# RWKV attention into a SoLU feed-forward on one core: a written-out order for the first chunks, constant products on TensorE, one row of u, and a reordered first pair

## The chip, the cores and the metric

The kernel runs on one core of a Trainium2 chip. The time is that of the device in microseconds, from launch to the end of the last instruction; lower is better. The core has five engines with a queue each, worked off strictly in program order: TensorE (PE, matrix products into PSUM), VectorE (DVE), ScalarE (ACT), GpSimd (POOL, which does not touch PSUM here) and SyncE (SP, which issues nearly all DMAs). They meet only through semaphores, so an instruction that waits holds up all that stands behind it on its engine.

## The reference

```python
# attention: r, k, v of shape (4, 8, 768, 48); w, u of shape (8, 48)
for t in range(S):
    cur = einsum('bhd,bhe->bhde', u[None] * kt, vt)
    y[:, :, t] = einsum('bhd,bhde->bhe', rt, state + cur)
    state = w[None, :, :, None] * state + einsum('bhd,bhe->bhde', kt, vt)
x = y.transpose(0, 2, 1, 3).reshape(3072, 384)
# feed-forward: w_in (384, 1024), w_out (1024, 384), g_ln (1024)
h = x @ w_in
e = exp(h - h.max(-1)); sm = e / (e.sum(-1) + 1e-9)
solu = h * sm
ln = (solu - mean(solu)) / sqrt(var(solu) + 1e-6) * g_ln
out = ln @ w_out
```

w_in, w_out and g_ln reach the chip as 64-bit floats and are converted there.

## The kernel before

**Chunks.** A unit of work is one batch and 128 tokens: 4 batches x 6 chunks are 24 units, numbered with the batch running fastest. "Chunk i" below is unit i. Inside a chunk the recurrence is a masked score matrix (r times decay, k times inverse decay, only later rows), plus the diagonal term with u; between chunks a state per batch is carried.

**Steps of a chunk, by name and line.** `load` (L472) brings k and r ("kr") and v. `turn_r` and `turn_k` (products L726 and L734) transpose r and k on TensorE; VectorE multiplies r by a table of powers (L727), ScalarE copies k (L736). `decay_k` and `decay_r` (L682, L689) multiply k and r by a table on GpSimd. `weigh` (L695, L696) forms k*u*r, on GpSimd but for chunk 0, where VectorE does it; `sum_own` (L700) sums it per head on VectorE; `diagonal` (L714) writes eight diagonal matrices on ScalarE. `whole_scores` (L749) are the score products, `take_scores` (L773) copies them under the mask over the diagonals on VectorE. `whole_y` (L800) gives the attention output, `take_y` (L849) copies it on ScalarE into xT, `whole_outer` (L874) gives the chunk's outer product and `update` (L895 to L901) adds it to the state. `ffn_in` (L909) is h = x @ w_in and ScalarE's exponential of it (L912). `unit` takes the reciprocal of the sum (L919), multiplies h by e (L921, VectorE) and centres and squares on ScalarE (L923, L924). `halve_ln` (L959) splits solu into 16-bit halves on ScalarE, `turn` has a DMA transpose them, `join_ln` (L953) puts them together again on VectorE; `ffn_out` (L991) multiplies by w_out, ScalarE scales the result (L993) and SyncE stores it. `deviation` (L930, L932) forms the scale on GpSimd.

**Weights.** They come in 14 pieces: six of w_in (512 KB each, three for each half of h's columns), eight of w_out (384 KB each). `load_weights` (L511) has six buffers. `convert_a` (L522, ScalarE), `convert_b` (L535, L537, VectorE), `convert_c` (L545, GpSimd) and for w_out `convert_d` (L552, VectorE) make 32-bit floats of one piece. For w_in `convert_b` puts its first result, `part`, into h's PSUM tile.

**The first stage** is a loop over i from -2 to 6. Iteration i works ahead: it turns chunk i+2, scores i+1, outputs i, and from i = 2 on runs the feed-forward of j = i-2; a table `conversions` says how many pieces each iteration converts. h of chunk 0 comes at the top of i = 2, with both halves together.

**The second stage** takes pairs of chunks, i = 7, 9, ... In it the scores are computed for 64-token halves: `scores` (L766), `within` (L828, the part of y inside a half), `carried` (L839, the part from the state and from `middle`, L883), `outer` (L865). `attend` does scores, outer, masked copies and `middle` for two chunks. From chunk 9 on k and r are transposed by DMA too: `halve_rk` (ScalarE L973, VectorE L974) splits them, `turn` transposes, `join_rk` (L953) joins. The first pair, i = 7, is marked `late` and has an order of its own: `ffn_in(5)`, `unit(5)` and `attend([7, 8])` first, then the rest of `decay`, then `sum_own(10)` and `halve_rk(10)`; `unit(6)` stands after `join_rk(10)` and `diagonal(10)`.

**PSUM** has eight banks: two for the scores, two for h, two in a ring "m" (y, outer product, o, tables), and one each for "ka" and "kb" (turn_r, turn_k, and the outer products of the pairs).

The order on every engine is that of the Python calls; no scheduler moves anything.

Of the kernel before, what the change touches and what calls it, by code (L numbers as in the profile page):

```python
# [399 lines left out]
def direct_path(  # L400
# [53 lines left out]
    psM = ctx.enter_context(tc.tile_pool(name="psM", bufs=2, space=PSUM))  # L454
# [13 lines left out]
    def load(i, which="krv"):  # L468
        b, c = units[i]
        for t, src, n in ((kpads, k, "k"), (rpads, r, "r"), (vts, v, "v")):  # L470
            if n in which:
# [14 lines left out]
    nc.scalar.dma_start(out=u_bc.rearrange("p h d -> p (h d)"),  # L486
                        in_=u.rearrange("h d -> (h d)").partition_broadcast(128))
# [37 lines left out]
    def convert_b(j):  # L525
        hi, low = step[j]
        n = low.shape[1]
        ma = wpool.tile([128, n], U32, tag="ma", name="ma", bufs=4)
        part = ma
        if pieces[j][2] is None:  # L530
            part = psH.tile([128, dff], F32, tag="h", name="part").bitcast(U32)[:, 0:n]

        nc.vector.tensor_scalar(out=part, in0=hi, scalar1=3, scalar2=0x3FFFFFF8,  # L535
                                op0=ALU.logical_shift_left, op1=ALU.bitwise_and)
        nc.vector.scalar_tensor_tensor(out=ma, in0=hi, scalar=0xC0000000, in1=part,  # L537
                                       op0=ALU.bitwise_and, op1=ALU.bitwise_or)
        step[j] = ma, low
# [30 lines left out]
    load(1, "kr")  # L570
    load_weights(1)
    load(2, "kr")
    load_weights(2)
    load_weights(3)
    load(0, "v")
    load(3, "kr")
    load_weights(4)
    load(1, "v")
    load_weights(5)
    load(4, "kr")  # L580
    load(2, "v")

    ident = const.tile([128, 128], F32, name="ident")
    make_identity(nc, ident)
    for vt in vts:
        nc.gpsimd.memset(vt[:, :, D:], 0.0)
# [21 lines left out]
    nc.tensor.transpose(wd_ps, wq.rearrange("a q d -> a (q d)"), ident[0:HP, 0:HP])  # L608
    nc.vector.tensor_scalar(out=pw[:, 0, 0], in0=wd_ps, scalar1=LOW, scalar2=HIGH,
# [112 lines left out]
    def turn_r(i):  # L722
        rT = factors(i)["rT"]
        ps = psM.tile([128, HP, T], F32, tag="ka", name="tr_ps", bufs=1)
# [4 lines left out]
    def turn_k(i):  # L729
        X = live[i]  # L730
        ps = psM.tile([128, HP, T], F32, tag="kb", name="tk_ps", bufs=1)
# [119 lines left out]
    def outer(chunks):  # L851
# [4 lines left out]
        kv = [psM.tile([128, 2, HP, D], F32, tag=f"k{'ab'[c]}", name="kv_ps", bufs=1)  # L856
# [47 lines left out]
    def ffn_in(i):  # L904
        X = live[i]
        h_ps = psH.tile([128, dff], F32, tag="h", name="h_ps")
        for n in range(dff // NX):
            for j in range(KD):
                nc.tensor.matmul(h_ps[:, ts(n, NX)], X["xT"][:, j, :], w_in_sb[:, j, ts(n, NX)],  # L909
                                 start=(j == 0), stop=(j == KD - 1))  # L910
        e = X["e"] = fpool.tile([128, dff], F32, name="e", bufs=1)
        nc.scalar.activation(out=e, in_=h_ps, func=ACT.Exp, accum_out=sums[:, i : i + 1])  # L912
        X["h"] = h_ps
# [84 lines left out]
    todo = list(range(len(pieces)))  # L998
    conversions = {-2: 1, -1: 1, 0: 2, 1: 2, 2: 2, 3: 2, 4: 2, 5: 2}
    now = []  # L1000
    for i in range(-2, LA + LO):
        j = i - LA
        if i == -1:
            nc.sync.dma_start(out=g_sb, in_=moe_g_ln.rearrange("(c p) -> p c", p=128))
        if 0 <= i:
            load(i + 5, "kr")
            load(i + 3, "v")
        if i >= LA:
            ffn_in(j)
        before, now = now, [todo.pop(0) for _ in range(conversions.get(i, 0))]  # L1010
        for p in before:
            if pieces[p][2] is not None:
                convert_c(p)
        if i == -2:
            turn_r(0)
            turn_k(0)
            turn_table(back, kdec, psM.tile([128, HP, 128], F32, tag="m", name="kd_ps"))
            weigh(0, nc.vector)
            decay_k(0)
            sum_own(0)  # L1020
        for p in now:
            convert_a(p)
            if ahead < len(pieces):
                load_weights(ahead)
                ahead += 1
        if -2 < i:
            turn_r(i + 2)
            if i >= LA:
                unit(j)
            if i < 0 or i >= LA:  # L1030
                sum_own(i + 2)
            turn_k(i + 2)
        if i < LA:
            for p in now:
                convert_b(p)
        if i == 0:
            sum_own(2)
        if i != 1:
            decay_k(i + 3)
            if i + 3 >= FIRST:  # L1040
                decay_r(i + 3)
            if i < 0:
                weigh(i + 3, nc.gpsimd)
        for p in now if i < LA else []:
            convert_c(p)
        if i == 1:
            weigh(3, nc.gpsimd)
            decay_k(4)
        if 1 <= i:
            weigh(i + 3, nc.gpsimd)  # L1050
# [8 lines left out]
        if 0 <= i + 1 < WHOLE:  # L1059
            whole_scores(i + 1)  # L1060
            take_scores(i + 1)
        if i < 0:
            diagonal(i + 2)
        if 0 <= i:
# [4 lines left out]
        if i == 1:  # L1069
            turn_table(fore, rdec, psM.tile([128, HP, 128], F32, tag="ka", name="rd_ps",  # L1070
                                            bufs=1))
            sum_own(3)
        if 0 <= i:
            diagonal(i + 2)
        if i == 1:
            nc.vector.tensor_single_scalar(out=minus_g, in_=g_sb, scalar=-1.0, op=ALU.mult)
        if i >= LA:
            for p in before:
                convert_d(p)
            for p in now:  # L1080
                convert_b(p)
# [28 lines left out]
    for i in range(LA + LO, N + LA + LO, 2):  # L1110
# [10 lines left out]
        if late:  # L1121
            decay(i + 3)
            ffn_in(j)
# [9 lines left out]
        if late:  # L1133
            sum_own(i + 3)
            halve_rk(i + 3)
# [26 lines left out]
        for n in (i, i + 1):  # L1162
            if n < N:
                update(n)
        for n in second:
# [5 lines left out]
        if j + 1 < N:  # L1171
# [57 lines left out]
```

## Time and profile before

| | |
|---|---|
| median of 6 runs | 353.93 us (351.54 to 354.68) |
| profiled execution: time / span | 351.09 us / 349.3 us |
| TensorE busy in the span | 329.4 us (94%) |
| VectorE, ScalarE, GpSimd busy | 206.3, 234.3, 169.1 us |
| DMA traffic | 52.88 MB, mean 151 GB/s |
| first product of h, chunk 0 | 27.63 us |
| first product of h, chunks 1 and 2 | 36.78 and 45.34 us |
| first product of h, chunk 8 | 117.53 us |

The page gives the busy share of each engine in 40 slices, the TensorE clock that was granted ("PEclk", ten tenths shown as 9), the chain of work that ended last, and groups of instructions. An order-of-time line reads: start, time taken, engine, line, operation, output and input tiles and shapes, number of instructions; in square brackets, how long the engine stood idle before it and what ended that. "PEld" is the load of a matrix that stays in the array. A 128x512 product in 32 bits counts as two instructions in the profile. The times of a chunk's steps are those of one execution, the profiled one.

### The profile page before, as it was taken

What the parts mean: (1) busy time and instruction counts of PE and PEld (TensorE: products, weight loads), DVE (VectorE), ACT (ScalarE), POOL (GpSimd) and SP (SyncE); (2) the same over time, 40 slices, a digit from 0 to 9 for tenths busy, and PEclk for the clock granted to TensorE, in tenths of its full rate; (3) what the DMA queues carried; (4) which work ended last, traced back from release to release, by engine and by line L of the source; (5) the groups of instructions that cost most, each with busy time, mean ns of one, the idle gap of its engine ahead of it and who ended that gap; (6) DMA issues with size and microseconds to landing.
All of it is one profiled execution on the core that took longest, in us unless ns stands there. A gap on an engine that the chain in (4) does not pass through costs nothing.

```text
span 349.3 us, 10540 instructions
## 1 busy us (share of the span) xinstructions
PE 329.4 (94%) x4443; PEld 196.0 (56%) x4443; DVE 206.3 (59%) x381; ACT 234.3 (67%) x476; POOL 169.1 (48%) x199
## 2 busy tenths in 40 slices
PE   2599999999999799999999999999999999999993
PEld 2485566656555365565565565565565555555563
DVE  7795888896476389459459369367256062233320
ACT  4765988988854895794794794796595465465510
POOL 4879667799949199466476475450300000000000
PEclk9769999999999999999999999999999999999999
DMA  7999998169999999969979979869823522554641
GB/s 170 262 223 196 258 213 133 29 115 178 145 237 165 173 210 174 194 150 163 158 173 165 164 160 155 147 139 188 187 79 65 129 75 56 127 127 97 136 98 42
DMA packets 164885, 52.88 MB, mean 151 GB/s; under 512 B 157917, under 2 KB 161245, under 8 KB 164829
## 3 DMA queue, kind: packets, MB, share of 16 engines
q1 hardware_dynamic: 164684, 51.92, 78.8%
q8 instruction: 37, 0.61, 0.8%
q10 hardware_dynamic: 144, 0.20, 0.2%
q14 instruction: 20, 0.16, 0.2%
HBM read 26.94 MB, written 4.72 MB: 91 GB/s over the span
## 4 chain that ended last, share of the span: by engine, by line
PE 77%; ACT 6%; DMA 6%; SPq 5%; DVE 3%; issue 2%; POOL 1%; ACTq 0%; DVEq 0%; POOLq 0%
PE o_ps L991 33%; PE h_ps L909 32%; DMA halves<-halves 4%; PE at L828 3%; PE at L839 3%; SPq L472 3%; PE at L766 2%; SPq L511 2%; DMA raw<-in_moe_w_in_dram 2%; DVE solu L921 2%; ACT AT L714 2%; PE kv_ps L865 2%; ACT halves L959 1%; ACT e L912 1%; PE y_ps L800 1%
## 5 line engine op out<-in xcount | busy, mean ns | idle before, releaser
L909 PE MATMUL h_ps<-w_in_sb,xT 128*128 128x512 f32 x288 | 129.8, 600 | 3.7 <-DVE solu L921 3.3
L991 PE MATMUL o_ps<-w_out_sb,lnT 128*128 128x384 f32 (+1 forms) x400 | 128.3, 476 | 0.0
L991 PEld LDWEIGHTS o_ps<-w_out_sb,lnT 128*128 128x128 f32 x400 | 74.3, 190 | 48.9 <-issue 4.3
L909 PEld LDWEIGHTS h_ps<-w_in_sb,xT 128*128 128x128 f32 x288 | 52.8, 190 | 63.4 <-issue 57.2
L912 ACT ACTIVATE e<-h_ps 128x1024 f32<-128x1024 f32 x24 | 24.5, 1022 | 38.0 <-PE h_ps L909 37.9
L923 ACT ACTIVATE solu<-solu,st 128x1024 f32<-128x1024 f32 x24 | 27.5, 1148 | 33.3 <-DVE solu L921 33.3
L959 ACT COPY halves<-solu 128x2048 uint16<-128x2048 uint16 x24 | 45.4, 1892 | 6.0 <-DMA halves<-halves 6.0
L899 POOL TENSOR_TENSOR state<-state,pw 48x192 f32<-48x192 f32 x32 | 22.6, 707 | 49.6 <-DVE state L895 47.8
L953 DVE COPY lnT<-halves 128x2048 uint16<-128x2048 uint16 x24 | 37.7, 1590 | 6.0 <-DMA halves<-halves 5.7
L930 POOL TENSOR_SCALAR st<-st 128x1 f32<-128x1 f32 x24 | 6.4, 265 | 64.2 <-ACT e L924 64.1
L682 POOL TENSOR_TENSOR kp<-kpad,kdec 128x512 f32<-128x512 f32 x24 | 32.0, 1334 | 6.0 <-ACT kdec L631 5.4
L714 ACT ACTIVATE AT<-same,own 128x64 f32<-128x64 f32 x136 | 34.3, 340 | 0.0
L695 POOL TENSOR_TENSOR rku<-kpad,u_bc 128x384 f32<-128x384 f32 x23 | 28.4, 1235 | 9.1 <-DVE own L700 9.1
L919 DVE RECIPROCAL st<-sums 128x1 f32<-128x1 f32 x24 | 3.8, 160 | 47.8 <-ACT e L912 47.5
L921 DVE SCALAR_TENSOR_TENSOR solu<-h_ps,st,e 128x1024 f32<-128x1024 f32 x24 | 30.8, 1284 | 2.1
L565 DVE TENSOR_REDUCE least<-mag 128x1 f32<-128x384 f32 (+1 forms) x14 | 8.5, 606 | 35.0 <-ACT mag L563 35.0
L953 DVE COPY rk<-halves 128x2048 uint16<-128x2048 uint16 x15 | 23.7, 1581 | 7.2 <-DMA halves<-halves 7.0
L696 POOL TENSOR_TENSOR rku<-rku,rpad 128x384 f32<-128x384 f32 x23 | 26.9, 1169 | 1.8
L993 ACT ACTIVATE o<-o_ps,st 128x384 f32<-128x384 f32 (+1 forms) x25 | 14.0, 558 | 18.5 <-PE o_ps L991 12.6
L924 ACT ACTIVATE e<-solu 128x1024 f32<-128x1024 f32 x24 | 25.4, 1057 | 0.8
L689 POOL TENSOR_TENSOR rp<-rpad,rdec 128x512 f32<-128x512 f32 x15 | 21.0, 1402 | 4.3 <-DVE halves L974 4.3
L773 DVE COPY_PREDICATED AT<-later_half,at 128x256 f32<-128x256 uint32 x34 | 12.3, 440 | 14.5 <-PE at L766 14.5
(101 smaller groups left out, 383.0 us busy)
## 6 DMA issues: line engine op xcount, KB each, us to landing
raw<-in_moe_w_in_dram SPq DMA_DIRECT2D x12, 512.0 KB, 4.8
raw<-in_moe_w_out_dram SPq DMA_DIRECT2D x16, 384.0 KB, 4.5
kpad<-in_k_dram SPq DMA_DIRECT2D x24, 192.0 KB, 4.8
rpad<-in_r_dram SPq DMA_DIRECT2D x24, 192.0 KB, 5.5
vt<-in_v_dram SPq DMA_DIRECT2D x24, 192.0 KB, 5.4
out_dram<-o SPq DMA_DIRECT2D x23, 192.0 KB, 3.7
halves<-halves SPq DMA_TRANSPOSE x39, 5.2
u_bc<-in_u_dram ACTq DMA_DIRECT2D x1, 192.0 KB, 3.1
```

Source lines behind the costliest of these rows:

```text
L682: nc.gpsimd.tensor_mul(X["kp"].rearrange("p h d -> p (h d)"), kpads[i % NLD].rearrange("p h d -> p (h d)"), kdec.rearrange("p a d -> p (a ...
L695: engine.tensor_mul(rku, kpads[i % NLD][:, :, 0:D], u_bc)
L696: engine.tensor_mul(rku, rku, rpads[i % NLD][:, :, 0:D])
L714: nc.scalar.activation(out=AT[:, h, :], in_=unit_matrix, func=ACT.Copy, scale=X["own"][:, h])
L909: nc.tensor.matmul(h_ps[:, ts(n, NX)], X["xT"][:, j, :], w_in_sb[:, j, ts(n, NX)], start=(j == 0), stop=(j == KD - 1))
L912: nc.scalar.activation(out=e, in_=h_ps, func=ACT.Exp, accum_out=sums[:, i : i + 1])
L921: nc.vector.scalar_tensor_tensor(out=solu, in0=X["h"], scalar=rs, in1=X["e"], op0=ALU.mult, op1=ALU.mult, accum_out=tot)
L923: nc.scalar.activation(out=solu, in_=solu, func=ACT.Identity, scale=-float(dff), bias=tot)
L924: nc.scalar.activation(out=X["e"], in_=solu, func=ACT.Square, accum_out=ss)
L953: nc.vector.tensor_copy(out=words.bitcast(U16).rearrange("p n (t o) -> p o n t", o=2), in_=turned)
L959: nc.scalar.copy(out=both.rearrange("p (o n) -> p o n", o=2), in_=split(X["solu"]))
L991: nc.tensor.matmul(o_ps, X["lnT"][:, f, :], w_out_sb[:, f, part], start=(f == 0), stop=(f == KF - 1))
```

## The change

**Order.** The iterations -2 to 1 and the feed-forward of chunk 0 are replaced by a list of calls. In it the six pieces of w_in are all converted ahead of the second half of h(0); `ffn_in` takes the halves of h's columns one at a time, the first half after the first four pieces have been converted; the output of chunk 2 and the turns of chunk 3 follow h(0); conversion of w_out begins with iteration 2. Conversions of a piece go through `take_up` (`convert_a`, then the next weight load). `weigh(0)` is on GpSimd.

**Loads.** v of chunk 0 and 1 are issued earlier, k and r of chunk 3 after the sixth weight piece, g_ln at the end of the list.

**Constant products.** `spin(n)` issues n products of the identity by itself into h's PSUM tile, whose result nobody reads; 19 in all, at six places.

**u.** It is loaded as one row; a product with a row of ones spreads it over 128 partitions in PSUM, and ScalarE copies it to `u_bc`.

**PSUM.** "ka", "kb" and "m" become one ring of four banks, into which `part` goes too.

**First pair.** `sum_own(10)` and `halve_rk(10)` stand ahead of `ffn_in(5)`; `unit(6)` stands after the state update, ahead of `join_rk(10)`.

```diff
-    psM = ctx.enter_context(tc.tile_pool(name="psM", bufs=2, space=PSUM))
+    psM = ctx.enter_context(tc.tile_pool(name="psM", bufs=4, space=PSUM))
...
-    nc.scalar.dma_start(out=u_bc.rearrange("p h d -> p (h d)"),
-                        in_=u.rearrange("h d -> (h d)").partition_broadcast(128))
+    u_row = u_bc[0:1].rearrange("p h d -> p (h d)")
+    nc.scalar.dma_start(out=u_row, in_=u.rearrange("h d -> (h d)").unsqueeze(0))
...
-            part = psH.tile([128, dff], F32, tag="h", name="part").bitcast(U32)[:, 0:n]
+            part = psM.tile([128, n], F32, tag="m", name="part").bitcast(U32)
...
     load(1, "kr")
+    load(0, "v")
     load_weights(1)
     load(2, "kr")
     load_weights(2)
+    load(1, "v")
     load_weights(3)
-    load(0, "v")
+    load_weights(4)
+    load_weights(5)
     load(3, "kr")
-    load_weights(4)
-    load(1, "v")
-    load_weights(5)
+    load(2, "v")
     load(4, "kr")
-    load(2, "v")
+    nc.sync.dma_start(out=g_sb, in_=moe_g_ln.rearrange("(c p) -> p c", p=128))
...
+    def spin(n):
+        ps = psH.tile([128, dff], F32, tag="h", name="spin")
+        for _ in range(n):
+            nc.tensor.matmul(ps[:, 0:128], ident, ident, start=True, stop=True)
+    spin(3)
...
+    u_ps = psM.tile([128, dm], F32, tag="m", name="u_ps")
+    nc.tensor.matmul(u_ps, ones_row, u_row, start=True, stop=True)
+    nc.scalar.copy(out=u_bc.rearrange("p h d -> p (h d)"), in_=u_ps)
+    spin(3)
...
-    def ffn_in(i):
+    def ffn_in(i, halves=(0, 1)):
         X = live[i]
-        h_ps = psH.tile([128, dff], F32, tag="h", name="h_ps")
-        for n in range(dff // NX):
+        if 0 in halves:
+            X["h"] = psH.tile([128, dff], F32, tag="h", name="h_ps")
+        h_ps = X["h"]
+        for n in halves:
...
+    turn_r(0)
+    turn_k(0)
+    turn_table(back, kdec, psM.tile([128, HP, 128], F32, tag="m", name="kd_ps"))
+    weigh(0, nc.gpsimd)
+    decay_k(0)
+    sum_own(0)
+    diagonal(0)
+    take_up(0)
+    spin(2)
+    whole_scores(0)
+    convert_b(0)
+    decay_k(1)
+    weigh(1, nc.gpsimd)
+    turn_r(1)
+    spin(4)
+    turn_k(1)
+    take_scores(0)
+    convert_c(0)
+    sum_own(1)
+    take_up(1)
+    diagonal(1)
+    spin(3)
+    whole_y(0)
+    whole_outer(0)
+    convert_b(1)
+    convert_c(1)
+    whole_scores(1)
+    update(0)
+    take_y(0)
+    decay_k(2)
+    weigh(2, nc.gpsimd)
+    turn_r(2)
+    take_up(2)
+    spin(4)
+    turn_k(2)
+    take_scores(1)
+    convert_b(2)
+    convert_c(2)
+    load(5, "kr")
+    load(3, "v")
+    whole_y(1)
+    whole_outer(1)
+    whole_scores(2)
+    take_up(3)
+    take_y(1)
+    convert_b(3)
+    convert_c(3)
+    sum_own(2)
+    ffn_in(0, (0,))
+    take_up(4)
+    convert_b(4)
+    convert_c(4)
+    load(6, "kr")
+    load(4, "v")
+    take_up(5)
+    diagonal(2)
+    convert_b(5)
+    convert_c(5)
+    ffn_in(0, (1,))
+    update(1)
+    take_scores(2)
+    decay_k(3)
+    whole_y(2)
+    whole_outer(2)
+    turn_r(3)
+    take_y(2)
+    turn_k(3)
+    unit(0)
+    weigh(3, nc.gpsimd)
+    decay_k(4)
+    turn_table(fore, rdec, psM.tile([128, HP, 128], F32, tag="m", name="rd_ps"))
+    update(2)
+    sum_own(3)
+    diagonal(3)
+    weigh(4, nc.gpsimd)
+
+    todo = list(range(6, len(pieces)))
     now = []
-    for i in range(-2, LA + LO):
+    for i in range(LA, LA + LO):
...
         if late:
             decay(i + 3)
+            sum_own(i + 3)
+            halve_rk(i + 3)
             ffn_in(j)
             unit(j)
             attend([i, i + 1])
...
-        if late:
-            sum_own(i + 3)
-            halve_rk(i + 3)
...
         for n in (i, i + 1):
             if n < N:
                 update(n)
+        if late:
+            unit(j + 1)
         for n in second:
             join_rk(n)
...
-        if j + 1 < N:
+        if j + 1 < N and not late:
             unit(j + 1)
```

## The prediction

> **What bounds the kernel now.** I read the page's slices first, then the busy time by stretch, then the chain that ended last, then the order of time at the start and in the first pair. Slices:
>
> ```profile
> PE   2599999999999799999999999999999999999993
> PEclk9769999999999999999999999999999999999999
> DMA  7999998169999999969979979869823522554641
> ```
>
> TensorE is full but for the start, slice 14 and the end. By stretch (length, then busy us and count of PE, PEld, DVE, ACT, POOL, then granted clock, DMA share, GB/s):
>
> ```profile
> 10.00:15.00 5.00, 2.88 (x40) 2.33 (x40) 3.00 (x6) 4.06 (x12) 4.82 (x5) 0.85 1.21 265
> 15.00:20.00 5.00, 4.00 (x44) 3.00 (x40) 4.89 (x9) 4.07 (x11) 4.92 (x5) 0.50 0.96 217
> 20.00:25.00 5.00, 5.00 (x106) 4.37 (x104) 4.67 (x9) 2.79 (x10) 4.23 (x4) 0.63 1.02 283
> 110.00:120.00 10.00, 7.40 (x113) 4.34 (x112) 3.81 (x5) 7.28 (x15) 4.57 (x4) 1.00 1.03 158
> 140.00:180.00 40.00, 40.00 (x543) 22.51 (x545) 23.92 (x40) 30.07 (x63) 22.20 (x24) 1.00 0.99 174
> ```
>
> From 120 to 330 us PE has no gap, so what is saved ahead of 117.5 us goes through to the end whole. The losses: PE idle before 45 us 10.97 us (4.76+2.21+2.12+1.00+0+0.40+0+0.48+0 over nine stretches of 5); the half clock 0.15 x 2.88 + 0.50 x 4.00 + 0.37 x 5.00 = 4.3; the first pair 0.21 + 0.71 + 2.60 = 3.5; the end 19.30 - 13.94 = 5.4. The rest, 325.2 us, is matmul work that the change does not touch. So at most 18.8 us is in play.
>
> Which of it can be had is read from the chain that ended last (start, us, what):
>
> ```profile
> 18.98 7.01 DMA raw<-in_moe_w_in_dram
> 26.07 0.73 ACT low L522
> 31.65 1.46 ACT AT L714 x5
> 36.78 5.39 PE h_ps L909 x12
> ```
>
> The start hangs on the sixth w_in piece, landed at 26.0, not on PE. In order of time (start, us, instruction, idle before it and who ended that):
>
> ```profile
> 12.76 0.66 PE L734 MATMUL tk_ps<-ident,kp 128*128 128x128 f32 x4 [1.83 <-POOL kp L682]
> 12.95 4.76 SPq L472 DMA_DIRECT2D rpad<-in_r_dram  x1
> 39.74 2.45 ACT L714 ACTIVATE AT<-ident,own 128x128 f32<-128x128 f32 x8
> 42.26 1.03 ACT L912 ACTIVATE e<-h_ps 128x1024 f32<-128x1024 f32 x1
> ```
>
> ScalarE reaches the exponential of chunk 1 only at 42.26, straight after eight diagonals: there ScalarE is as full as PE. And the first pair:
>
> ```profile
> 91.66 6.79 SPq L948 DMA_TRANSPOSE halves<-halves  x2
> 104.94 6.21 SPq L948 DMA_TRANSPOSE halves<-halves  x2
> 111.06 1.90 ACT L959 COPY halves<-solu 128x2048 uint16<-128x2048 uint16 x1 [5.19 <-DMA halves<-halves]
> 117.53 5.42 PE L909 MATMUL h_ps<-w_in_sb,xT 128*128 128x512 f32 x12 [2.60 <-DVE solu L921]
> ```
>
> The 2.60 us is no fault of VectorE: chunk 7's exponential stands on ScalarE behind a split (L959) that waits for a transpose issued at 104.94.
>
> **The change, part by part.**
>
> *Spins.* 3+3+2+4+3+4 = 19 products of 128x128. Nearest rows: four transposes of that size in 1.06-1.12 us at the half clock, 0.60-0.66 at the full one. So 19 cost 2.1 to 4.1 us, put where PE waits (1.83 and 0.99 us for kp, more at the start): nothing on the path; without that cover, all of it. Do they buy clock? [...] But either way PE waits for others in 10-25 us, so the 4.3 us of half clock are mostly not on the path: I count 0 in this execution (bounds 0 and -1.7, about 3.4 us of half clock falling on h).
>
> *u as one row.* The 128-row load goes (192 KB), a product of 128x384 (0.33 us by 5.43/16 of L991, doubled at half clock) and a ScalarE copy (0.5 us, like L849) come, both ahead of 6 us where these engines idle: free. The DMA engines lose about 0.6 us of work.
>
> *weigh(0) to GpSimd.* 1.1 us (0.55+0.56) leaves VectorE, 2.0 us (L695+L696) comes to POOL at 5.7-7.7, where POOL idles until kdec at 10.0: hidden with 2 us to spare. [...] The table products (L620, the last two 1.12 us) run just then. [...]
>
> *Loads.* Until the sixth w_in piece has landed, SyncE now issues kr0-3, v0-1, w0-5 and u: 5.3 MB in 2.5 to 26.0, 225 GB/s. After: kr0-2, v0-1, w0-5: 4.72 MB, so 21.0 + 2.5 = 23.5; by intervals (v0 landed at 11.76+6.9 = 18.7, r3 at 12.95+7.4 = 20.4, so kr3 took 1.7; u's 128 packets of 62-79 ns on 16 engines 0.6) 26.0 - 1.7 - 0.6 = 23.7. I take 23.6, bounds 22.7 (1.7 us for a w piece, 1.05 for the others, counted from r0's landing at 6.4) and 26.0 (no gain). The moved kr3, v2, kr4 then land by about 28; w6 and w7 by 33, before ScalarE wants them at 37.8.
>
> *The written-out order.* By the waits in the built program the chain is: w5 23.6; low (L522, 0.68) 24.3; eight diagonals of chunk 2, now behind it on ScalarE, 26.8; two masked copies (L773, 1.35) 28.2; y and outer of chunk 2 (1.08+0.52, overlapping) 29.7; transposes 30.1; rT (0.69) 30.85; unit(0) on VectorE (0.2+1.28) 32.4. h(0) itself ends at about 27.8 instead of 33.05, five us early, but that is not the gain: ScalarE then does solu, square (2.3), rdec 0.62, diagonals of chunk 3 2.45, two low 1.02, kT 0.47, diagonals of chunk 4 2.45: 41.7, and the exponential of chunk 1, 42.26 now. From there to h(2) is 2.64 (42.26 to 44.90 now): 44.4, against 45.34. **Gain 0.9 to 1.1**, one for one with the landing; I take 1.1 (the early part of the walk may save 0.2 of latencies). Behind that exponential wait solu(1), h(2) and with it all later PE work; from h(2) on PE is the limit again (h(3) ready 1 us before PE).
>
> *PSUM pool.* One ring of four banks for ka, kb, m and `part`: the built program's waits on the path are met by readers that finish earlier (turn_r(4) by rT of chunk 3, turn_k(4) by kT of chunk 3). 0.
>
> *First pair.* sum_own(10) and halve_rk(10) go ahead of h(5). On VectorE they wait for rku(10), which POOL ends at 82.1, and unit(5), now at 81.11, is queued behind: 82.1+0.55+0.69 = 83.3, solu to 84.8, four masked copies to 86.3. The product of the split scores (L828), now at 84.84, waits for them: +1.5 us of PE idle. The transposes do not start earlier: SyncE issues nine loads until 91.6 and then the transpose, in both. unit(6) ahead of join_rk(10), which waits until 98.47, gains: its solu goes from 99.86 to 95.5; ScalarE's work on it leaves the stretch 101-103, so the split of chunk 11 is ready at 103.1 instead of 104.9, SyncE is free at 104.05 (99.64+3.86+out), both transposes start 0.9 us earlier, and h(8) starts at 116.65. PE, late by 0.7 at h(7) (102.0), has 1 us idle left there, so the 1.5 is absorbed. **Gain 0.9**, bounds +1.5 (the stall passes on) and -2.6 (all of the gap).
>
> **Sum.** Profiled execution: span 349.3, time 351.09, so 1.8 around it. 349.3 - 1.1 - 0.9 = 347.3, time 349.1. The median of the six, 353.93, lies 2.84 above that execution. Carried over whole: 351.9. Some of the 2.84 I put on the start, where clock and landings differ from run to run: with more of h(0) at half clock (up to 1.7) the change would spare it. I choose 0.6 of it: **351.3**.
>
> **Rivals.**
> (a) *Slower*: the sixth piece lands late. Low and the diagonals of chunk 2 stand behind it on ScalarE and everything after behind them, +1 us per us. Even is 23.6 + 2.0 = 25.6, half a per cent slower from 27.4. At 185 GB/s (slices of 170 and 196 occur) 4.72 MB land at 28.0: 353.93 + 4.4 - 2.0 = 356.3. Against it: 262 and 258 in other early slices.
> (b) *No change*: the small pieces, not bytes, cost the DMA, it lands at 24.7, and the first pair's stall passes on while the transposes stay: 0 +- 1.5, 353.9. For it: the 4.76 us in which SyncE was held at a load of 192-byte rows.
> (c) *More*: landing at 22.7, no stall in the first pair, and half-clock runs cured: -1.1-0.9-0.9-1.5-0.6 = -5.0, 348.9.
>
> **How the numbers follow.** Forecast 0.50, (a) 0.10, (b) 0.22, (c) 0.18. Half a per cent, 1.8 us, is about what this measurement tells from no change. The forecast's own range is 349.5 to 352.8 (landing and pair bounds), some four fifths of it under 352.15: 0.41, with (c) and a little of (b) 0.64; slower (a) and a little of (b), 0.13; same 0.23. The range leaves out the far half of (a) and of (c): 348.0 to 354.8.
>
> **What would show it.** w5 landing near 23.6; h(0) ending near 28 but h(2) starting near 44.3, with PE idle 2 us ahead of it and the exponential of chunk 1 directly behind the diagonals of chunk 4; the clock at 1.00 from about 10 us; L828 of the first pair with 1.5 us idle; the last idle before h(8) about 1 us. The prediction is wrong if h(2) comes without a gap ahead of it, or if h(8) still waits 2.6 us.

## The result, and the profile after

The changed kernel takes 350.87 us (median of 21 executions, 348.62 to 354.69), the kernel before 353.32 beside it (42 executions, 350.74 to 355.30). The ratio is 0.9929, 95% interval [0.9907, 0.9950]: faster by 0.7%, with 351.3 us forecast. Ratios here leave out executions more than 1.5% above the fastest of their kernel (two of these 21, four of twelve of e4_fill and one of e3_pair_only below); medians are over all.

The two profiled executions do not show this gain: 351.35 us (span 349.6) after, 351.09 (349.3) before. That is the first thing to explain. The page's slices of the kernel after:

```profile
PE   8989799998999899999999999999999999999993
...
PEclk9999989999999999999999999999999999999999
```

The start is filled. The clock row shows 9 throughout the first slices (its first record is at 10.8 us; until then the products last as long as at half clock, four transposes 1.09 us at 6.49 against 0.66 at 11.40), where before had 7 and 6 in the second and third. But slice 5 (counted from 0, 43.7 to 52.4 us) has an 8, where before had a 9. Order of time on TensorE around it (start, us, instruction, and in brackets the idle time before it and who ended it):

```profile
32.87 5.42 PE L926 MATMUL h_ps<-w_in_sb,xT 128*128 128x512 f32 x12
41.01 0.52 PE L889 MATMUL kv_ps<-vt,kp 128*32 128x48 f32 x32
43.50 7.08 PE L926 MATMUL h_ps<-w_in_sb,xT 128*128 128x512 f32 x12 [1.97 <-DVE solu L939]
54.42 5.42 PE L926 MATMUL h_ps<-w_in_sb,xT 128*128 128x512 f32 x12
```

h(1) starts 3.9 us earlier than before (36.78), h(2) 1.84 earlier (45.34), and h(3) only 0.17 earlier (54.59): h(2) took 7.08 us in place of 5.42. Cut at the edges of the recorded clock, by stretch (length, PE busy and count, granted clock, DMA share, GB/s):

```profile
38.06:41.48 3.42, 3.42 (x105) 1.00 1.25 250
41.48:44.89 3.41, 1.44 (x10) 1.00 1.07 235
44.89:48.30 3.41, 3.41 (x6) 0.50 1.12 232
48.30:51.72 3.42, 3.42 (x30) 1.00 1.34 232
```

The clock is halved for one stretch of 3.41 us, right behind the one that holds the idle 1.97 us. Half of 3.41 is 1.7 us, what h(2) lost. ScalarE from the sixth w_in piece on: its conversion, the exponential of chunk 0, and, as the prediction had it, diagonals of chunk 4 with the exponential of chunk 1 directly behind them:

```profile
23.15 0.68 ACT L522 ACTIVATE low<-raw 128x512 uint32<-128x512 uint32 x1 [0.79 <-DMA raw<-in_moe_w_in_dram]
...
27.91 1.02 ACT L931 ACTIVATE e<-h_ps 128x1024 f32<-128x1024 f32 x1 [1.74 <-PE h_ps L926]
...
38.38 2.45 ACT L729 ACTIVATE AT<-ident,own 128x128 f32<-128x128 f32 x8
40.74 1.00 ACT L931 ACTIVATE e<-h_ps 128x1024 f32<-128x1024 f32 x1
```

The first pair on TensorE: the wait before the masked products has come, the one before h(8) has shrunk from 2.60 us:

```profile
86.24 1.80 PE L843 MATMUL at<-AT,vt 64*32 64x64 f32 x128 [1.50 <-DVE AT L788]
...
117.17 5.42 PE L926 MATMUL h_ps<-w_in_sb,xT 128*128 128x512 f32 x12 [1.44 <-DVE solu L939]
```

From h(5) to h(8) it is 45.00 us after (72.17 to 117.17) and 45.18 before (72.35 to 117.53). The rest, from h(8) to the end, is 232.4 against 231.8 us.

**What the medians say.** Every execution comes with its mean granted clock. At 0.998 or more stand 7 of the 21 executions after, median 349.25 us, and 18 of 63 before (those beside the experiments), median 351.60: with the clock held, the change is worth 2.35 us. The others stand at 351.75 and 353.17. (These are few executions, chosen by their clock.) So the profiled execution after is one that had gained about 2 us and lost 1.7 of it to the clock. Theory to be tested: *the start gains 1 to 2 us; an idle stretch of about 2 us costs, by chance, another 1.7 us behind it.* Rivals: the gain is the constant products' (clock), or the first pair's.

### The profile page after: what moved, and what is told of

Same layout as the page of the kernel before. It is cut to its first block, busy times and chain, and to the rows that moved or that the text cites. A ratio compares the mean times of both kernels' runs of the same rounds, so it can differ in the third digit from the quotient of the medians.

```text
span 349.6 us, 10620 instructions
## 1 busy us (share of the span) xinstructions
PE 335.8 (96%) x4483; PEld 200.6 (57%) x4483; DVE 208.1 (60%) x379; ACT 234.6 (67%) x477; POOL 171.4 (49%) x202
## 4 chain that ended last, share of the span: by engine, by line
PE 72%; DVE 7%; POOL 7%; ACT 6%; DMA 4%; issue 3%; ACTq 0%; POOLq 0%; DVEq 0%
PE o_ps L1009 31%; PE h_ps L926 29%; DMA halves<-halves 4%; PE at L843 3%; PE at L854 3%; ACT AT L729 2%; PE at L781 2%; DVE solu L939 2%; POOL kp L697 2%; POOL rku L711 2%; PE kv_ps L880 1%; DVE ma L537 1%; POOL rku L710 1%; PE y_ps L815 1%; POOL w_in_sb L545 1%
## 5 line engine op out<-in xcount | busy, mean ns | idle before, releaser
L926 PE MATMUL h_ps<-w_in_sb,xT 128*128 128x512 f32 x288 | 131.8, 608 | 3.7 <-DVE solu L939 3.6
L971 DVE COPY lnT<-halves 128x2048 uint16<-128x2048 uint16 x24 | 38.7, 1628 | 7.7 <-DMA halves<-halves 7.5
L948 POOL TENSOR_SCALAR st<-st 128x1 f32<-128x1 f32 x24 | 5.0, 209 | 64.2 <-ACT e L942 64.1
L710 POOL TENSOR_TENSOR rku<-kpad,u_bc 128x384 f32<-128x384 f32 x24 | 29.6, 1232 | 9.9 <-DVE own L715 9.0
L697 POOL TENSOR_TENSOR kp<-kpad,kdec 128x512 f32<-128x512 f32 x24 | 31.1, 1299 | 4.2 <-DMA kpad<-in_k_dram 1.9
L711 POOL TENSOR_TENSOR rku<-rku,rpad 128x384 f32<-128x384 f32 x24 | 28.2, 1176 | 1.9
L971 DVE COPY rk<-halves 128x2048 uint16<-128x2048 uint16 x15 | 25.3, 1687 | 3.1 <-DMA halves<-halves 2.9
L704 POOL TENSOR_TENSOR rp<-rpad,rdec 128x512 f32<-128x512 f32 x15 | 23.6, 1571 | 1.8 <-DVE halves L992 1.8
```

What stands on the lines that cost most here:

```text
L697: nc.gpsimd.tensor_mul(X["kp"].rearrange("p h d -> p (h d)"), kpads[i % NLD].rearrange("p h d -> p (h d)"), kdec.rearrange("p a d -> p (a ...
L710: engine.tensor_mul(rku, kpads[i % NLD][:, :, 0:D], u_bc)
L711: engine.tensor_mul(rku, rku, rpads[i % NLD][:, :, 0:D])
L971: nc.vector.tensor_copy(out=words.bitcast(U16).rearrange("p n (t o) -> p o n t", o=2), in_=turned)
```

## The experiments

The kernels ran in three sets (e1 to e4, e5 to e8, f1 to f3 with e9), each beside executions of the kernel before. The last column counts executions whose mean clock is 0.993 or less: as an estimate, at least one half-clock stretch (3.41 us at half clock take 0.005 from the mean over 349 us) besides the last few us of the kernel, where the clock falls in every profile (by itself 0.001 to 0.005 of the mean). It is a lower bound: the profiled execution after has such a stretch and stands at 0.994.

| kernel | median us | ratio to before, 95% | executions at 0.993 or less |
|---|---|---|---|
| the change | 350.87 | 0.9929 [0.9907, 0.9950] | 9 of 21 |
| e1_no_spin | 352.03 | 0.9968 [0.9937, 1.0000] | 5 of 12 |
| e2_start_only | 352.61 | 1.0006 [0.9975, 1.0037] | 11 of 12 |
| e3_pair_only | 351.94 | 0.9985 [0.9956, 1.0015] | 3 of 12 |
| e4_fill | 351.98 | 0.9941 [0.9900, 0.9983] | 5 of 12 |
| e5_unit1_early | 347.94 | 0.9879 [0.9844, 0.9914] | 4 of 6 |
| e6_split10_later | 353.01 | 1.0010 [0.9979, 1.0041] | 11 of 12 |
| e7_exp7_early | 349.13 | 0.9904 [0.9868, 0.9940] | 1 of 6 |
| e8_all | 345.49 | 0.9795 [0.9765, 0.9826] | 0 of 5 |
| f1_six_ahead | 346.04 | 0.9800 [0.9765, 0.9835] | 0 of 6 |
| f2_twelve_ahead | 348.89 | 0.9871 [0.9831, 0.9910] | 3 of 6 |
| f3_all_no_spin | 345.69 | 0.9786 [0.9748, 0.9823] | 2 of 6 |

### The parts of the change

**e1_no_spin**: the change without the constant products.

```diff
     def spin(n):
+        return
```

> The changed kernel without its 19 constant products; everything else, the written-out order too, is kept, and the output is complete. The prediction counted the products at 0 us. If that holds: 350.9 us, ratio to the kernel before 0.993, whatever the clock does before 25 us, since TensorE waits for others there. Rival, the clock: the gain is the constant products' work. Then the granted clock between 5 and 25 us falls back to about 0.6 to 0.8 as in the kernel before, products of h(0) and h(1) fall into it, and the time goes back to 352.5 to 354 us (ratio 0.998 to 1.002).

352.03 us lies between the two expectations, and the interval reaches from close to the first into the second. In its profiled execution TensorE waited 2.20 us before h(2), with no loss, and 2.27 us before h(8), which then took 7.11 us. The scatter of these waits hides in the time what the products do; the trace shows it. Without the four products that stood ahead of chunk 2's transpose at 19.2 us, TensorE waits 2.76 us there for GpSimd (1.17 us in the change), the window from 16.66 us is 0.26 busy, and the next, 20.08 to 23.49 us, is at half clock. It falls on the work ahead of h(0):

```profile
19.77 1.70 PE L816 MATMUL y_ps<-AT,vt 128*32 128x128 f32 x32
...
22.04 1.77 PE L765 MATMUL at<-rk 48*64 48x128 f32 x32
23.75 5.42 PE L927 MATMUL h_ps<-w_in_sb,xT 128*128 128x512 f32 x12
```

In the change these start at 19.76, 21.11 and 22.13 us. h(0) comes 1.62 us later and h(2), at 44.79, 1.29 later, although the sixth piece's conversion starts 0.13 earlier. That is the rival's mechanism, in one execution; f3 below weighs the products again.

**e2_start_only** and **e3_pair_only**: the two parts apart (e3 is the same edit the other way round, made in the kernel before).

```diff
             decay(i + 3)
-            sum_own(i + 3)
-            halve_rk(i + 3)
             ffn_in(j)
...
             check_sums()
+        if late:
+            sum_own(i + 3)
+            halve_rk(i + 3)
...
-        if late:
-            unit(j + 1)
         for n in second:
             join_rk(n)
...
-        if j + 1 < N and not late:
+        if j + 1 < N:
             unit(j + 1)
```

> The changed kernel with the first pair put back as it was (own sums and split of chunk 10 after the scores, unit 6 after the exponential's place of before). In the profiled executions the first pair gained 0.36 us at h(8) (117.53 to 117.17). If the start carries the gain: 351.2 us, ratio 0.994. If the first pair carries it, as a rival has it: 353 us, ratio 0.999.

> The kernel before with the change of the first pair alone. If the start carries the gain: 353.0 us, ratio 0.999, the masked products of the first pair wait about 1.5 us for VectorE as they do in the changed kernel, and h(8) starts at 117.2 us. If the first pair carries it: 351 us, ratio 0.993 to 0.995. By the prediction's 0.9 us for this part: 352.4 us, ratio 0.9975.

Neither part alone makes a difference that can be measured, and both together make 0.7%. Waits that simply add up would give that only at the edges of both intervals. The profiled execution of e2 is its second fastest (349.97), with the clock full but for the end:

```profile
43.64 5.39 PE L926 MATMUL h_ps<-w_in_sb,xT 128*128 128x512 f32 x12 [1.96 <-DVE solu L939]
52.85 5.42 PE L926 MATMUL h_ps<-w_in_sb,xT 128*128 128x512 f32 x12
115.72 5.42 PE L926 MATMUL h_ps<-w_in_sb,xT 128*128 128x512 f32 x12 [3.51 <-DVE solu L939]
```

The start's gain is there (h(2) 1.70 us earlier than before, h(3) 1.74), and h(8) starts 1.81 earlier. But the first pair's wait stands in one piece of 3.51 us, and 11 of 12 executions have a low clock, with 352.61 as the median, 2.6 us above this one. In e3 the pair's waits were 1.50 us before the masked products and 2.47 before h(8), and h(5) to h(8) took 46.0 us (45.2 before): the pair's part by itself saved nothing.

**e4_fill**: seven constant products ahead of h(2), in a buffer of the ring "m".

```diff
+        if i == LA + 2:
+            ps = psM.tile([128, 128], F32, tag="m", name="fill")
+            for _ in range(7):
+                nc.tensor.matmul(ps, ident, ident, start=True, stop=True)
         if i > LA:
             ffn_in(j)
```

> The changed kernel with seven constant products of 128x128 ahead of h(2), in a buffer of their own, so that TensorE works through most of the 1.97 us in which it stood idle from 41.5 to 43.5 us. Theory of the gap: the idle time before h(2) is what brought the clock down to 0.67 in 45 to 50 us; filled, h(2) starts at 43.5 us and takes 5.4 us in place of 7.1, the granted clock of 45 to 50 us is 1.00, h(3) starts at 52.7 in place of 54.4 and the time is 349.2 us (ratio 0.989). Rival: the low clock has another cause (a budget of work since the start, or chance): h(2) takes 7 us again, or at another place as long, and the time stays at 350.9 us (0.993), or gets longer by what the products delay.

In the profiled execution (349.14 us) the gap is gone, h(2) takes 5.42 us from 44.24 and h(3) starts at 53.49, 0.9 us ahead of the change. But the executions run from 348.45 to 355.63, five of twelve with a low clock, and only one has a profile. What the others lost is not seen. The gap theory holds in this trace, and the time leaves it open.

### Waits taken away at their cause

**e5_unit1_early**: the diagonals of chunk 4 go behind the exponential of chunk 1, unit 1 ahead of two conversions.

```diff
         if i > LA:
             ffn_in(j)
+        if i == LA + 1:
+            diagonal(4)
+            unit(j)
...
-        if i > LA:
+        if i > LA + 1:
             unit(j)
...
-        diagonal(i + 2)
+        if i != LA:
+            diagonal(i + 2)
```

> The changed kernel with two groups of instructions in another place: the eight diagonals of chunk 4 on ScalarE behind the exponential of chunk 1 in place of ahead of it, and unit 1 on VectorE ahead of two conversions and of the factor rT of chunk 5. The prediction's chain says that the exponential of chunk 1 is held up by ScalarE's diagonals alone. If so the exponential starts at about 38.4 us, when h(1) is done, h(2) follows the outer products without a gap at 41.6 in place of 43.5, no window of TensorE falls under half busy there, h(3) starts at 51.0 (54.4 with the half clock, 52.7 without), and 1.9 to 3.4 us come through to the end: 347.5 to 349.0 us, ratio 0.983 to 0.988. Rival: the gain is lost to GpSimd, which is 97% busy from 70 to 90 us, and to the transposes of the first pair: h(3) is early but h(8) stays at about 117 us and the time at 350.9 (0.993).

```profile
38.17 1.02 ACT L931 ACTIVATE e<-h_ps 128x1024 f32<-128x1024 f32 x1
39.18 2.44 ACT L729 ACTIVATE AT<-ident,own 128x128 f32<-128x128 f32 x8
```

The exponential starts at 38.17, h(2) at 41.99 after an idle 0.67 us (unit 1 waits for VectorE's conversions until 40.65), h(3) at 51.24, 3.2 us ahead of the change. From chunk 0's exponential to h(2) it is 14.30 us, in the change 15.59: the edit is worth 1.29 us there, the clock 1.7. h(8) starts at 114.17, 347.94 us in all: as expected, and the rival (lost again in the first pair) falls. One wait is left, 1.77 us before the masked products at 83.32; the window that held it was 0.47 busy, and the next ran at half clock. Four of the six executions have a low clock.

**e6_split10_later**: the own sums and the split of chunk 10 behind the scores.

```diff
             decay(i + 3)
-            sum_own(i + 3)
-            halve_rk(i + 3)
             ffn_in(j)
             unit(j)
             attend([i, i + 1])
+            sum_own(i + 3)
+            halve_rk(i + 3)
```

> The changed kernel with the own sums and the split of chunk 10 behind unit 5 and the scores of the first pair (their place of before), unit 6 staying early. Theory of the two waits: the split's place only shares out one wait between the masked products at 85 us and h(8), and the clock decides: the 1.5 us ahead of the masked products go, the wait ahead of h(8) grows from 1.4 to 2.6 us or more, long enough for half a window of clock to be lost behind it, and the time is 351.5 to 353 us (ratio 0.996 to 1.001). Rival (sum of waits): what is saved at 85 us is saved at the end: 349.4 us, ratio 0.989.

The time is 353.01 us, at the upper edge of what the theory of the two waits gave: a wait taken away, and 2.1 us lost. The rival (349.4) falls. TensorE in the profiled execution (the slowest of the twelve), and the windows behind the pair:

```profile
45.09 7.08 PE L926 MATMUL h_ps<-w_in_sb,xT 128*128 128x512 f32 x12 [1.99 <-DVE solu L939]
118.85 8.14 PE L926 MATMUL h_ps<-w_in_sb,xT 128*128 128x512 f32 x12 [3.48 <-DVE solu L939]
```

```profile
114.13:117.54 3.41, 1.23 (x89) 1.00 1.04 180
117.54:120.95 3.41, 2.10 (x3) 0.50 1.16 175
120.95:124.37 3.42, 3.42 (x5) 0.50 1.54 183
124.37:127.78 3.41, 3.41 (x9) 1.00 0.87 158
```

The 1.5 us before the masked products are gone and the wait before h(8) is 3.48 us, as in e2. The next window begins with the rest of the gap and at half clock, and a second one follows: h(8) takes 2.7 us more. In e2's trace a wait as long brought no loss, but 11 of 12 executions of each have a low clock, 9 of 21 of the change. So the pair's part saves hardly any waiting (h(5) to h(8) is 45.1 us in e2 and e6, 45.0 in the change); it leaves two waits of about 1.5 us in place of one of 3.5, and no wait of that length is followed by a half-clock window in any trace here.

**e7_exp7_early**: for the second pair, chunk 7's exponential goes ahead of the split that waits for a transpose, unit 7 ahead of two joins.

```diff
+        if j == LO + 2:
+            ffn_in(j)
         decay(i + 4)
...
+        if j == LO + 2:
+            unit(j)
         join_ln(l + 1)
...
         if j < N and not late:
-            ffn_in(j)
-            unit(j)
+            if j > LO + 2:
+                ffn_in(j)
+                unit(j)
             within([i, i + 1])
```

> The changed kernel with the exponential of chunk 7 ahead of the split of chunk 4 and of the diagonals of chunk 11 on ScalarE, and unit 7 on VectorE ahead of two joins. The prediction says that h(8) waits for chunk 7's exponential behind a split that waits for a transpose. If so the exponential starts at about 107.5 us in place of 114.4, h(8) follows the products with the state without a wait at 115.8 in place of 117.2, and 1.4 us come through: 349.4 us, ratio 0.989. Rival: another late transpose takes the wait over (a join of chunk 11, or the split of chunk 4, now later, for its own output products behind h(8)): TensorE then waits at another place between 115 and 140 us, and the time stays at 350.9 (0.993).

```profile
106.75 1.02 ACT L931 ACTIVATE e<-h_ps 128x1024 f32<-128x1024 f32 x1 [3.74 <-PE h_ps L926]
...
109.78 1.90 ACT L977 COPY halves<-solu 128x2048 uint16<-128x2048 uint16 x1 [1.92 <-DMA halves<-halves]
```

The exponential is out of the way at 107.8, h(8) follows without a wait at 114.93, and no wait of over 0.6 us appears later. h(5) to h(8) is 43.5 us, 1.5 less than in the change. 349.13 us, as expected: the late transpose held up h(8) only because the exponential stood behind it. (Part of the 1.7 us between the medians may be the clock's: one low execution of six here, 9 of 21 there.)

**e8_all**: the three edits of e5, e6 and e7 in one kernel; of each, the line that carries it:

```diff
+            diagonal(4)
+            unit(j)
...
+            sum_own(i + 3)
+            halve_rk(i + 3)
...
+        if j == LO + 2:
+            ffn_in(j)
```

> The three edits together: chunk 1's exponential ahead of chunk 4's diagonals, chunk 10's split behind the scores, chunk 7's exponential ahead of the split of chunk 4. If the waits of TensorE at 41.5, 85 and 115.7 us are each ended by the instruction named and nothing else is near, all three go: 1.9 + 1.5 + 1.4 = 4.8 us, and up to 1.7 us more where the clock was halved behind a gap: 344.5 to 346.1 us, ratio 0.974 to 0.980, h(8) at 111 to 112.5 us. Rival: the first pair is bound by GpSimd and by the transposes, so that what the start gives is lost there: h(8) not before 114.5 us and 348 us or more, ratio 0.985.

345.49 us, 345.02 to 346.37: as expected, faster than both kernels (0.9795 to before; 0.9795/0.9929 = 0.987 to the change), and its five executions scatter by 1.35 us where the 21 of the change scatter by 6. The page's slices:

```profile
PE   7989999999999999999999999999999999999993
...
PEclk9999999999999999999999999999999999999999
```

h(2) starts at 42.63, h(8) at 111.27, and after 20 us the longest wait is 0.66 us. The split of chunk 10, bad alone (e6), is harmless here: no wait is left before h(8) for it to lengthen. What it adds to e5 and e7 was not measured apart.

### The clock by itself

**f1_six_ahead** and **f2_twelve_ahead**: e8_all with some of chunk 4's diagonals ahead of the exponential of chunk 1 again, so that the gap before h(2) can be chosen. f2 writes four of them twice.

```diff
+        if i == LA + 1:
+            diagonal(4, range(8))     # f1: range(6)
+            diagonal(4, range(4))     # f1: not there
         if i > LA:
             ffn_in(j)
         if i == LA + 1:
-            diagonal(4)               # f1: range(6, 8) in its place
             unit(j)
```

> The kernel with the three edits, with six of chunk 4's eight diagonals put back ahead of the exponential of chunk 1, so that h(2) comes later by a chosen bit: six by 0.305 us is 1.83, of which 1.1 us is slack, since VectorE takes up unit 1 only at 41.03 us while the exponential ends at 39.94. TensorE's gap ahead of h(2) becomes 0.66 + 0.7 = 1.4 us. Theory of the window (clock windows of 3.41 us on a grid that doesn't follow the kernel; a window that is busy for about 0.4 or less is followed by one at half clock): 1.4 us leave any window at least 0.59 busy, so no clock is lost, and the time is 345.5 + 0.7 = 346.2 us, with as small a spread as without. Rival (any gap over about 1 us can bring the clock down): single executions are 1.7 us longer, 347 to 348 us.

> As f1_six_ahead with all eight diagonals of chunk 4 ahead of the exponential, and four of them written a second time with the same values: twelve by 0.305 us less 1.1 us of slack make h(2) 2.55 us late, a gap of 3.2 us. Theory of the window: about 2 us of idle time in one window are enough, so that a gap of 3.2 us does it in about 8 of 10 positions of the grid (contained: 0.2 of 3.41 us of positions; cut by an edge with at least 2 us on one side: 2 x 1.2 us; 2.6/3.41), and costs 1.7 us behind it: most executions at 345.5 + 2.55 + 1.7 = 349.7 us with h(2) 7.1 us long, a few at 348.0. Rival (a gap costs its own length): 348.0 us.

The theory's 3.41 us and its share of about 0.4 are read from the traces of before and of e1 to e8: windows 0.26 and 0.40 (e1), 0.36 (e6) and 0.39 (before) busy were each followed by one at half clock. f1: gap 1.36 us, its window 0.60 busy and the next at full clock, h(2) 5.42 us long, 346.04 us, all six executions within 1.2 us: the 0.70 us by which the gap is longer than e8's, or 0.55 by the medians, is all that shows, and no execution is 1.7 us late. f2: gap 3.13 us, 2.47 longer than e8's; 348.89 us, 3.4 more than e8, six executions from 347.14 to 350.98. So the long gap costs about 0.9 us above its length, and scatters by 3.8 us; expected were 1.4 above its length on average, and six executions cannot tell 0.9 from that. In the profiled one, the slowest, two windows ran at half clock, and h(2) took 8.31 us:

```profile
40.41:43.82 3.41, 1.24 (x64) 1.00 1.25 236
43.82:47.23 3.41, 2.45 (x3) 0.50 0.89 204
47.23:50.65 3.42, 3.42 (x5) 0.50 1.30 233
```

**f3_all_no_spin**: e8_all with the edit of e1.

```diff
     def spin(n):
+        return
```

> The kernel with the three edits, without the 19 constant products, in order to weigh them where the waits further back add no scatter. By the prediction (0, since TensorE waits for others before 25 us): 345.5 us. Rival: without them windows at 10 to 20 us are under 0.4 busy, as one at 16.7 us was in the changed kernel without them, and a half-clock window falls on h(0) or the work ahead of it, which TensorE, full from 20 us, hands on: 346.5 to 347.5 us.

345.69 against 345.49 us: no difference, but with intervals of 0.3 to 0.4% each up to about 1 us could hide. Its profiled execution has one half-clock stretch at 18.76 to 22.17 us, where TensorE was 0.91 busy; h(0) starts at 23.46 in place of 22.71, h(2) at 43.20 in place of 42.63, h(8) at 112.30 in place of 111.27. So the rival's half-clock window came, and was handed on as far as h(8). The spans are 344.4 to e8's 344.6 all the same: e8 took 1.3 us more from h(8) on, of which a wait of 0.51 us at 138 us is a part and the rest is not explained. Whether the products are worth anything in the time stays open below 1 us.

**e9_kr3_before_w4**, a single execution: the loads of chunk 3 back ahead of the fifth piece. It took 350.51 us; one execution says little about the time, so the trace counts here.

```diff
     load_weights(3)
+    load(3, "kr")
     load_weights(4)
     load_weights(5)
-    load(3, "kr")
```

> The changed kernel with the loads of chunk 3 back ahead of the fifth w_in piece, in one look at the trace. The prediction says that the landing of the sixth piece sets ScalarE's chain and through it h(2), one for one. Then the conversion of that piece starts 1.7 us later, at 24.9 in place of 23.15, the exponential of chunk 1 at 42.4 in place of 40.74 and h(2) at 45.2 in place of 43.5 us. Rival (ScalarE's chain is full by itself and the landing has slack): the exponential stays at 40.7 to 41.2 and h(2) at 43.5 to 44.

```profile
24.42 0.69 ACT L522 ACTIVATE low<-raw 128x512 uint32<-128x512 uint32 x1 [0.97 <-DMA raw<-in_moe_w_in_dram]
25.00 2.44 ACT L729 ACTIVATE AT<-ident,own 128x128 f32<-128x128 f32 x8
28.48 1.02 ACT L931 ACTIVATE e<-h_ps 128x1024 f32<-128x1024 f32 x1 [1.05 <-PE h_ps L926]
...
41.49 1.01 ACT L931 ACTIVATE e<-h_ps 128x1024 f32<-128x1024 f32 x1
```

The conversion starts 1.27 us later than in the change, the exponential of chunk 0 0.57, that of chunk 1 0.75, h(2) 0.76 (44.26). Neither expectation: 0.6 us for each us of landing. ScalarE's idle time before the exponential of chunk 0, in which it waits for h(0), goes from 1.74 to 1.05 us. The end of h(0) is what counts, as the traces of four kernels with one and the same start show, in which the pieces landed at different times:

| | conversion of the sixth piece | exponential of chunk 0 | h(2) | from the exponential to h(2) |
|---|---|---|---|---|
| the change | 23.15 | 27.91 | 43.50 | 15.59 |
| e2 | 23.12 | 28.05 | 43.64 | 15.59 |
| e7 | 24.05 | 28.83 | 44.43 | 15.60 |
| e6 | 24.69 | 29.49 | 45.09 | 15.60 |

Where the last three pieces came late together (e7, e6) h(2) did move one for one: 0.93 us for 0.90, 1.59 for 1.54. In e9 only the last two came late, and GpSimd had time to spare: in the change it converts the fifth and the sixth piece without a pause (24.08 to 26.69 us), here it stands idle for 0.46 us between them. The last products of h(0) wait for its last conversion:

```profile
26.34 1.12 PE L926 MATMUL h_ps<-w_in_sb,xT 128*128 128x512 f32 x2 [0.66 <-POOL w_in_sb L545]
27.67 1.13 PE L926 MATMUL h_ps<-w_in_sb,xT 128*128 128x512 f32 x2 [0.20 <-POOL w_in_sb L545]
```

(These are from e7; in the change no single wait is that long, and h(0) takes 5.74 us in place of 5.42.) The four also show by how much h(2) differs from one execution to the next: 1.6 us.

## Why the prediction was right, point by point

- *Spins, 0 us.* Not refuted by the time (f3 against e8, within about 1 us), but the reason fails in the traces: "PE waits for others in 10-25 us" leaves out that the products fill such a wait, and that an emptier window was followed by one at half clock, on work that h(0) waits for (e1: 0.26 busy, h(0) 1.62 us late, about the bound of 1.7; f3: 0.53 busy, 0.75 us). The products also cost more than the 2.1 to 4.1 us counted, 7.3 us by their rows: the row taken for them was that of transposes, of which four took 1.06 us where two constant products did. For the first full clock they were not needed in these traces. Before, TensorE had nothing but transposes in the window from 6.64 to 10.06 us (0.81 busy), and from 10.06 the clock was full: four transposes took 1.06 us at 8.34 and 0.63 at 10.29. In e1, with transposes from 6.51 to 9.23 us, then score products, it came between 9.3 and 10.6 us: four took 1.06 us at 8.24 and 0.63 at 10.64.
- *u as one row, weigh(0) on GpSimd, 0 us each.* Right, though u's product took 1.61 us (0.33 to 0.66 were counted) and k*u*r ended at 8.29 us, not 7.7; both lie before kdec (9.32 to 9.91 us), and TensorE waits for neither. Beside GpSimd's products (5.65 to 8.29 us) VectorE's last two table products took 1.79 us in place of 1.12.
- *Loads, sixth piece at 23.6.* Right: its conversion starts at 23.15 (26.07 before), and at 23.12 to 24.69 in the other kernels with this start.
- *Chain to h(2), 44.4, gain 1.1, "one for one with the landing".* The size fits: 43.50 in the profiled execution, 44.2 on average over the four kernels with this start, a gain of 1.3 (45.34 and 45.57 without it, before and in e3). "One for one" holds where the last three pieces move together. One link is wrong. "h(0) itself ends at about 27.8, five us early, but that is not the gain": it did end at 27.8, and it is the gain. The prediction let chunk 2's output wait for the masked copies behind the diagonals (28.2); they were done at 27.28, and the output started at 27.80, behind h(0). From there on ScalarE's order is as written, but its 9.3 us from solu to the exponential of chunk 1 were 8.77, because its rows overlap by about 0.1 us each (diagonals of chunk 4 from 38.38 to 40.83, the exponential from 40.74).
- *"PE idle 2 us ahead of h(2)".* Right, 1.97, and priced at nothing beyond itself: **this step failed.** The prediction wrote "the clock at 1.00 from about 10 us" beside a gap that it had itself foreseen. In the profiled execution the gap cost 1.66 us more and ate the start's gain; by the mean clock at least 9 of 21 executions lose a stretch somewhere, which need not be at this wait. In f2, where the gap was made longer, the time grew by about 0.9 us more than the gap.
- *First pair, 0.9.* The stall of 1.5 us before the masked products is right, and the transposes did start earlier (103.60 in place of 104.94; 0.9 was forecast). But they took 7.08 us in place of 6.21, so that 0.36 of it came through, and h(8) kept 1.44 us of wait, not 1. h(5) to h(8) shrank by 0.2 us. e2 and e6 show what the part is worth instead: with the start in place and the pair's wait in one piece of 3.5 us, 11 of 12 executions have a low clock (9 of 21 with it in two pieces), and the median is 1.7 to 2.1 us higher (352.61 and 353.01 to 350.87). So the part is worth about 2 us beside the start, by the clock, as these counts say, and not by the 0.9 us of waiting that the prediction counted.
- *Sum: -2.0 in the span.* With the clock held it is 2.35 us by the executions. That the median came out so near (350.87 for 351.3) is partly luck: the pair's 0.9 us did not come as waiting saved, the clock was counted nowhere behind the start, both kernels lose clock in a part of their executions, and the 0.6 us that the prediction gave to "half-clock runs" was a choice.
- The 0.6 us between h(8) and the end (232.4 and 231.8) is not explained; in the other profiled kernels that stretch is 231.8 to 233.4, less any clock lost at h(8).

## What to carry to other kernels

Where TensorE sets the time, price a wait by its length and by what it may do to the clock. In the fourteen traces here, behind 30 us, none of nine waits of 1.36 to 1.56 us was followed by a half-clock window, and six of thirteen from 1.77 to 3.51 us were, at up to 1.7 us a window. So one long wait was worth splitting here even where the sum of waits stayed the same (e2 and e6 against the change), and two changes must be tried together before either is given up: start and pair measured 0 apart and 0.7% together. A wait that a trace shows before a product is best undone on the engine that ends it: moving one exponential ahead of eight diagonals and another ahead of a split that waits for a transpose (e8, with chunk 10's split moved back) took away 5.4 us more by the medians, twice what the whole change did, and most of the scatter with it. And one trace is not enough to call a size wrong: the same start put h(2) at 43.50 to 45.09 us in four.

## What the runs showed of the hardware

Until the last stretch of a kernel, the granted clock changes in these traces only at multiples of 3.41 us from one another (at 13.47 and 23.71 us before, 44.89 and 48.30 in the change, 45.86, 49.27, 117.54 and 124.37 in e6), at another offset in each execution: counted back in steps of 3.41, the grid begins at 0.52 us in the change, 1.49 in e6 and 3.23 before. A wait of 1.97 us was enough for a half-clock window behind it where it lay within one window. The four kernels with one start have the same gap before h(2), 1.96 to 1.99 us. In the change and e6 it fell into one window (0.42 busy in both) and half clock followed. In e2 and e7 an edge cut it, and none did (e7):

```profile
39.70:43.11 3.41, 2.76 (x100) 1.00 1.30 236
43.11:46.52 3.41, 2.09 (x5) 1.00 1.12 151
```

Windows under 0.6 busy at full clock, as the grid of each trace cuts them, up to 120 us:

| busy share of the window | the next window |
|---|---|
| 0.26 (e1, 16.7 us), 0.36 (e6, 114.1), 0.36 (f2, 40.4), 0.39 (before, 10.1), 0.40 (e1, 115.7), 0.42 (after, 41.5), 0.42 (e6, 42.5), 0.47 (e5, 80.9), 0.53 (f3, 15.4) | half clock |
| 0.41 (e2, 110.8), 0.51 (before, 115.9), 0.56 (e2, 114.2), 0.56 (e3, 83.5), 0.57 to 0.58 (six windows in e4, e5, e7, e9, f1, f2 near 16 us, and others) | full clock |

The two rows overlap between 0.41 and 0.53, so the busy share of the records is not quite what decides; which products were in the window may count, and that is open. (In the change the window from 3.93 to 7.34 us, by the same grid, was busy throughout (3.41 us), with u's one-row product, constant products and transposes, and the next four transposes still took the 1.06 us of half clock.) Back to full it took a fuller window here: in before, e6 and f2, windows of 0.62 to 0.89 at half clock were followed by another at half clock, and one of 0.91 (f3) was not.

As an estimate, a gap of 1.97 us fits wholly into a window in (3.41 - 1.97)/3.41 = 0.4 of the offsets. The count of 9 in 21 cannot check this, since it takes in every wait of the kernel. That the offset makes the difference for the gap before h(2) is what these four traces show, and e1 and e9 fit (2.20 and 2.14 us, both cut by an edge, no loss). For the rest of the scatter between executions it is argued: only one execution of each kernel has a trace.
